# Attention and gated MLP on one core: row maxima ten pairs of units ahead instead of eleven, z's order in the rows, two pools for the gate

## The chip, the cores and the metric

The kernel runs on one core of one Trainium2 chip. The engines' names are those of the profile: PE is TensorE (its matrix products, PEld its weight loads), DVE is VectorE, ACT is ScalarE, POOL is GpSimd, SP is SyncE, from which most DMAs are issued. The metric is the device time of one execution in microseconds (us); the median of several runs is compared.

## The reference

```python
h = x + A(layernorm(x), wqkv, wo)
h2 = h + B(layernorm(h), w_in, w_sp, b_sp, w_out)

def A(x, wqkv, wo):                    # S=2048, D=512, 32 heads of Dh=16
    q, k, v = split(x @ wqkv)
    p = softmax(einsum("bhqd,bhkd->bhqk", q, k) * Dh ** -0.5)
    return einsum("bhqk,bhkd->bhqd", p, v) @ wo

def B(x, w_in, w_sp, b_sp, w_out):     # F=1376, Fh=688
    z = gelu(x @ w_in)
    z1, z2 = z[..., :Fh], layernorm(z[..., Fh:])
    g = einsum("ts,bsf->btf", w_sp, z2) + b_sp[None, :, None]
    return (z1 * g) @ w_out
```

Inputs and results are float32.

## The kernel before, in words

Most products in the projections and in the MLP are made of numbers split into a high and a low float16 part, and take three products (`mm3`, L108, L109, L110: high by high, high by low, low by high). In five engines' queues the order of instructions from the projections to the end of the rows is written by hand (`manual_schedule`): what stands behind a waiting instruction on its engine waits as well.

**Projections.** A loop of 24 projections of q and k (j = 0 to 23), twelve products each; the results are drained by VectorE (L461, L462). Into them are put the *row maxima* of the first scores. A softmax subtracts its row maximum before the exponential, and here the maxima are found from separate, smaller products, ahead of the scores: `max_pair(m)` makes eight steps, each one product (L224) into a bank of PSUM and an operation on it, six on VectorE alone (L229, one maximum each), and one pair of steps on ScalarE (absolute values, L234) and VectorE (L238). Eight m are a group of 512 queries of four heads. At its end `finish` reduces the group (L243) and splits it on GpSimd (L246 to L248), and `max_rows` turns it (L260), writes it to memory (L261, `m_scr`) and reads it back in two transfers (L264) into two rows of q, so that the scores' product subtracts the maxima. `ahead(k)` takes the next k steps during a projection, up to LEAD m in all.

**Attention.** There are 512 units (8 groups of four heads, 4 query blocks of 512, 16 key blocks), taken in pairs, 256 in all. Each pair follows the list `PAIR`: `s0` to `s7` are the eight score products (L801, in `product`), each with an exponential on ScalarE (L810); `M0` to `M7` are the eight steps of maxima for the pair that is LEAD pairs further on; `H` and `P` multiply weights by v (`weigh`, L826), for the pair before and the present one; `join` is `finish`, `turn` is `max_rows`, `out` copies a finished output from PSUM (`take`, L836), and `invert` makes the reciprocals of the sums. In the first pair there is nothing to weigh; four products with v as both operands (L1128, which the profile records as eight) stand there. The last LEAD pairs have no maxima left to make: the first of these follows `PAIR` without them, the others go through `scores2`, two products with one exponential of double width. Among these lie the beginnings of the next stage: rows of the output are loaded (`load_o`), scaled and split (`split_o`: ScalarE L735, VectorE L736), multiplied by wo (`make_h`, L743), 12 products one by one (`some_h`), and added to x (L747), with statistics (L750).

**Rows.** Sixteen rows of 128 positions in pairs (sb from the upper and the lower half). For each: `make_h` and `split_o` of later rows, `scale_h` and `minus_mean` (VectorE's small steps L754, L115 to L127, L764) for h of the row two further on; `make_z` four times (12 products of 344 columns each, L108 to L110, and a Gelu on ScalarE, L1206); `turn` transposes the next row (ScalarE L99, VectorE L105); statistics of z (L1268, L1219), and `gate_z` normalises z (L1222) and forms seven combinations of blocks for the gate. `parts` splits each of them into high (cast, L1210, ScalarE or GpSimd) and low (subtraction, L1211, VectorE or GpSimd).

**Gate and output.** The spatial product with w_sp is made from seven block products (A, C, B in turn; `product`, L108 to L110 with g). Their PSUM tiles come from one pool of four banks. ScalarE reads A with L1397 into p1 before t2 is added onto A. Then come the products with w_out.

Of the kernel before, what the change touches and what calls it, by code (L numbers as in the profile page):

```python
# [8 lines left out]
F32 = mybir.dt.float32  # L9
# [4 lines left out]
AF = mybir.ActivationFunctionType  # L14
# [18 lines left out]
KS = 48  # L33
LEAD = 11
KM = 50
PB = 6
FIRST = 2
RG = 64
# [21 lines left out]
def block_kernel(ctx: ExitStack, tc: tile.TileContext, x, wqkv, wo, w_in, w_sp4, b_sp, w_out, out):  # L60
# [209 lines left out]
    with ExitStack() as pre:  # L270
# [397 lines left out]
        for j in range(24):  # L668
            b, n, i = 1 + j // 8, j // 2 % 4, 1 - j % 2

            def between(d):
                if d == 1 and j >= FIRST:
                    ahead(5 if j < FIRST + 4 else 4)
                if d == 2 and takes:
                    takes.pop(0)()
                    if rest:
                        rest.pop(0)()
                if d == 3 and turned and done[0] % 8 > 3:
                    max_rows()
# [51 lines left out]

    def split_o(sb):
        o = os_.pop(sb)
        o2s[sb] = [e2.tile([P, DB, P], F16, name=f"o2{i}", bufs=1) for i in range(2)]
        nc.scalar.activation(o2s[sb][0], o, AF.Copy, scale=o_up)  # L735
        nc.vector.scalar_tensor_tensor(o2s[sb][1], o, o_up, o2s[sb][0], op0=ALU.mult, op1=ALU.subtract)  # L736
# [47 lines left out]
    with ExitStack() as at:  # L784
# [274 lines left out]
        for n in range(0, len(units), 2):  # L1059
# [38 lines left out]
            if len(later) == 2:  # L1098
                if turned:
                    max_rows()  # L1100
                more_h = n in (492, 494, 508, 510)
                scores2(hg, qb, kb, 0)
# [10 lines left out]
            for tok in PAIR if len(later) < 2 else ():  # L1113
# [10 lines left out]
                elif tok == "H" and prev is None:  # L1124
                    if first:
                        pv[0] = ps_v.tile([P, 512], F32, name="pv")
                        for j in range(4):
                            nc.tensor.matmul(pv[0][32 * j:32 * j + 32, :], vst[0][:, :32],  # L1128
                                             vst[0][:, :512], start=True, stop=True)
                    first = False  # L1130
                elif tok == "H":
# [12 lines left out]
            if len(later) == 2 and kb == 6:  # L1144
                invert()
            if n in (476, 480, 504, 508):
                asked.append(load_o(h_rows[{476: 0, 480: 1, 504: 2, 508: 3}[n]]))
            if n in (484, 488, 508):
                asked.pop(0)()
            if n in (488, 500, 510):  # L1150
                split_o(h_rows[(n - 488) // 11])
            if n == 500:
# [27 lines left out]
    with ExitStack() as mid:  # L1180
# [28 lines left out]
        def parts(name, k, src, eh, el):  # L1209
            (nc.gpsimd.tensor_copy if eh == "pool" else nc.scalar.copy)(T[name][0][:, k, :], src)  # L1210
            (nc.gpsimd if el == "pool" else nc.vector).tensor_sub(T[name][1][:, k, :], src, T[name][0][:, k, :])  # L1211

        def gate_z(sb, meanwhile):
# [28 lines left out]
            parts("t3", k, b12, "pool", "pool")  # L1242
            parts("b21", k, b21, "act", None)
            e.tensor_sub(t2, b21, t2)
# [3 lines left out]
        with tc.manual_schedule(engines={E.PE, E.Activation, E.DVE, E.Pool, E.SP}):  # L1248
# [3 lines left out]
            for k in range(NB):  # L1252
# [4 lines left out]
                if k + 3 < NB:  # L1257
                    split_o(row[k + 3])
                if new is not None:
                    mv, rs = scale_h(new)  # L1260
                    nb = minus_mean(e2, mv, rs)
                new_z(sb)
                make_z(sb, 1, 0)
                if k + 1 < NB:
                    turn(row[k + 1])
                make_z(sb, 1, 1)
                for c in range(2):
# [23 lines left out]
    with ExitStack() as fin:  # L1291
# [3 lines left out]
        ps_o = fin.enter_context(tc.tile_pool(name="fin_o", bufs=2, space=PSUM))  # L1295
        ps_g = fin.enter_context(tc.tile_pool(name="fin_g", bufs=4, space=PSUM))
        WB = len(FB) - 1
# [75 lines left out]
        with tc.manual_schedule(engines={E.PE, E.Activation, E.DVE, E.Pool, E.SP}):  # L1373
# [10 lines left out]
            for p in range(HB):  # L1384
# [5 lines left out]
                bt, bb = bias_up[:, p:p + 1], bias_up[:, p + HB:p + HB + 1]  # L1390
                A, C, B = [ps_g.tile([P, 512], F32, name="g")[:, :FC] for _ in range(3)]
                p1, v, q5 = [f2.tile([P, FC], F32, name=n) for n in ("p1", "v", "q5")]
# [73 lines left out]
```

## Time and profile before

| what | us |
|---|---|
| median of 3 runs (lowest, highest) | 1733.11 (1732.75, 1733.4) |
| the profiled execution's own time | 1732.66 |
| its span in the profile | 1730.9 |
| projections, 98 to 161.9 | 63.9 |
| first attention pair, to 167.46 | 5.56 |
| attention pairs with maxima, to 1250.25 | 1082.79 |
| the last 11 pairs, to 1295.57 | 45.32 |
| rows, to 1456.14 | 160.57 |
| gate and output, to 1731 | 274.86 |

Times in the rows of the profile count from the span's start. A timeline row has its start, its length, the engine, the line, the operation with output and inputs, and, in brackets, how long the engine was idle ahead of it and what ended that. A row of the groups view has line, engine, operation, shapes and count, then busy time in us and mean in ns, and the idle time ahead of the group with its cause. The windows view has start and end, length, and for each engine busy us and count of instructions, then the granted clock of PE (1.00 is full), the busy share of the DMA engines and GB/s. SPq is the queue of SP's DMAs.

### The profile page before, as it was taken

The numbers are of one execution on the slowest core, as the hardware profiler recorded it, in microseconds if no ns is written. First come the engines' busy times: TensorE is split into PE (matmuls) and PEld (weight loads), VectorE is DVE, ScalarE is ACT, GpSimd is POOL, SyncE is SP. The second block draws the span as 40 slices with busy tenths as digits, with TensorE's granted clock in tenths as the row PEclk, the third lists the DMA queues.
The fourth block names the chain that finished last, engine by engine and source line by source line (L and its number), as shares of the span: only waits on it lengthen the run. The fifth ranks groups of instructions, "written<-read, shape, count | busy, mean of one in ns | idle before, by whom it ended". The sixth has DMA issues, their size and how long they took to land.

```text
span 1730.9 us, 36558 instructions
## 1 busy us (share of the span) xinstructions
PE 1713.6 (99%) x13581; PEld 676.1 (39%) x13581; DVE 1389.4 (80%) x2896; ACT 1301.3 (75%) x2566; POOL 824.8 (48%) x1088
## 2 busy tenths in 40 slices
PE   9999999999999999999999999999999999999999
PEld 4433222222222222222222222222226666777776
DVE  7688999999999999999999999999927776111112
ACT  4334999999999999999999999999995554011000
POOL 1231867776672267877677767600004665100110
PEclk9999999999999999999999999999999999999999
DMA  5534332342231244445345434410125454743440
GB/s 183 162 97 143 101 88 74 98 100 73 75 71 29 63 124 134 139 125 150 92 141 139 133 111 128 108 23 9 45 58 143 131 172 149 274 148 132 171 173 25
DMA packets 185482, 196.13 MB, mean 113 GB/s; under 512 B 65960, under 2 KB 134632, under 8 KB 185304
## 3 DMA queue, kind: packets, MB, share of 16 engines
q1 hardware_dynamic: 183000, 188.16, 37.0%
q10 hardware_dynamic: 2304, 5.64, 0.9%
q8 instruction: 106, 1.74, 0.4%
q14 instruction: 72, 0.59, 0.1%
HBM read 124.92 MB, written 68.75 MB: 112 GB/s over the span
## 4 chain that ended last, share of the span: by engine, by line
PE 72%; DVE 15%; POOL 4%; ACT 3%; DMA 2%; issue 2%; SPq 1%; ACTq 0%; POOLq 0%; DVEq 0%
PE pv L826 24%; PE s L801 16%; PE m L224 9%; DVE mx L229 7%; PE g L108 4%; PE g L110 4%; PE g L109 4%; PE acc L108 3%; PE acc L110 3%; PE acc L109 3%; DMA rc<-r_scr 2%; DVE ab L238 1%; POOL op L1003 1%; ACT pt L810 1%; DVE og L836 1%
## 5 line engine op out<-in xcount | busy, mean ns | idle before, releaser
L810 ACT ACTIVATE pt<-s 128x512 f32<-128x512 f32 x1968 | 1006.9, 638 | 4.7 <-PE m L224 3.6
L229 DVE TENSOR_REDUCE mx<-m 128x1 f32<-128x512 f32 x1510 | 947.2, 682 | 12.8 <-PE m L224 3.9
L801 PE MATMUL s<-qst,kst 50*128 50x512 f16 x2048 | 604.4, 379 | 0.4
L826 PE MATMUL pv<-pt,vst 128*32 128x256 f32 (+1 forms) x6056 | 598.1, 466 | 4.1 <-DVE og L836 0.7
L224 PE MATMUL m<-kst,qst 48*128 48x512 f16 x1510 | 452.3, 381 | 0.0
L801 PEld LDWEIGHTS <-kst 50*128 50x128 f16 x2048 | 131.9, 94 | 352.1 <-issue 322.7
L826 PEld LDWEIGHTS pv<-pt,vst 128*32 128x32 f32 x6056 | 119.5, 108 | 289.9 <-issue 276.6
L224 PEld LDWEIGHTS <-qst 48*128 48x128 f16 x2048 | 159.3, 93 | 173.7 <-issue 123.8
L224 PE MATMUL m<-uvs,qst 48*128 48x512 f16 x504 | 190.7, 380 | 0.0
L238 DVE CUSTOM_DVE_ANT_0 ab<-m,ab 128x512 f32<-128x512 f32 x252 | 170.3, 676 | 2.7 <-ACT ab L234 2.7
L234 ACT ACTIVATE ab<-m 128x512 f32<-128x512 f32 x252 | 157.7, 626 | 16.5 <-PE m L224 15.8
L246 POOL TENSOR_SCALAR nm<-nm 128x16 f32<-128x16 f32 x32 | 6.5, 204 | 331.4 <-DVE nm L243 331.4
L1335 ACT ACTIVATE pT<-tp 128x384 fp32r<-128x384 f32 x32 | 14.0, 488 | 142.0 <-PE tp L1327 142.0
L1413 POOL TENSOR_TENSOR pr<-pr,z 128x344 f32<-128x344 f32 x8 | 7.3, 910 | 193.1 <-DVE pr L1412 181.7
L1003 POOL TENSOR_TENSOR op<-raw,op 128x512 f16<-128x512 f32 x80 | 92.8, 1160 | 5.8
L910 POOL TENSOR_TENSOR raw<-raw 128x512 f32<-128x512 f32 (+1 forms) x84 | 83.1, 989 | 6.7
L915 POOL TENSOR_TENSOR acc_sp<-acc_sp,raw 128x512 f32<-128x512 f32 x63 | 80.4, 1276 | 4.5
L110 PE MATMUL acc<-wi,hT 128*128 128x344 f16 x256 | 79.2, 309 | 2.1 <-DVE hT L105 2.1
L1357 DVE TENSOR_TENSOR y<-acc,h 128x512 f32<-128x512 f32 x16 | 11.1, 691 | 85.9 <-PE acc L1353 84.5
L108 PE MATMUL acc<-wi,hT 128*128 128x344 f16 x256 | 79.1, 309 | 0.0
L109 PE MATMUL acc<-wi,hT 128*128 128x344 f16 x256 | 79.1, 309 | 0.0
L907 POOL TENSOR_SCALAR raw<-raw 128x512 f32<-128x512 f32 (+1 forms) x88 | 52.1, 592 | 19.7 <-DMA raw<-in_wqkv 12.4
(227 smaller groups left out, 2269.3 us busy)
## 6 DMA issues: line engine op xcount, KB each, us to landing
raw<-in_w_sp SPq DMA_DIRECT2D x128, 256.0 KB
s_scr<-op SPq DMA_DIRECT2D x64, 256.0 KB
op<-s_scr SPq DMA_DIRECT2D x32, 512.0 KB
a_scr<-op SPq DMA_DIRECT2D x48, 256.0 KB
op<-a_scr SPq DMA_DIRECT2D x24, 512.0 KB
o_scr<-og SPq DMA_DIRECT2D x64, 128.0 KB
qst<-q_scr SPq DMA_DIRECT2D x192, 32.0 KB
kst<-k_scr SPq DMA_DIRECT2D x48, 128.0 KB
```

Of the source, the lines that this page charges most:

```text
L108: nc.tensor.matmul(ps, lh, rh, start=first, stop=False, **kw)
L109: nc.tensor.matmul(ps, lh, rl, start=False, stop=False, **kw)
L110: nc.tensor.matmul(ps, ll, rh, start=False, stop=last, **kw)
L224: nc.tensor.matmul(acc, q[r, p, c], keys[r, p], start=True, stop=True)
L229: nc.vector.reduce_max(at(t, e if t else e - 1), acc, axis=AX.X)
L234: nc.scalar.activation(ab[0], acc, AF.Abs)
L238: nc.vector.tensor_tensor_reduce(ab[0], acc, ab[0], 0.5, LOW, ALU.add, ALU.max, at(0, 0))
L801: nc.tensor.matmul(s, kst[hg % 2][r, p, kb * P:(kb + 1) * P], qst[hg * NQ + qb][r, p, :], start=True, stop=True)
L810: nc.scalar.activation(pts[p, kb][:, t, :], s, AF.Exp, scale=scales_[hg // 2])
L826: nc.tensor.matmul(pv[0][32 * j:32 * j + 32, a:b], vst[hg % 2][:, c:c + 32], pts[j % 2, kb][:, j // 2, a:b], start=kb == 0, stop=kb == NB - 1,
L910: pool.tensor_mul(got[0] if n else acc, got[0], got[0])
L1003: chores.append((lambda: pool.tensor_sub(t[0][:, 1], of(), t[0][:, 0]), TT))
```

## The change

LEAD falls from 11 to 10 and FIRST rises from 2 to 4; every projection from j = 4 on takes four steps of maxima (20 groups of four), where j = 2 to 5 took five and j = 6 to 22 four. One attention pair more has maxima, and one `scores2` pair less is there. The four products of v in the first pair are gone. The times at which the early rows are loaded, multiplied, split and made shift by a few units, the list of pairs that take an additional step of h has six places where it had four, and the split of three early rows is by VectorE (a tensor_scalar) where it was by ScalarE. In the rows, `scale_h` and `minus_mean` move behind the first `make_z` and the next row's `turn`; the subtraction for the low part of b21 is kept and issued there too, in the row after, except in the last. The gate takes its PSUM tiles from two pools of two banks in the order that the pool of four gave, but in other banks.

```diff
-LEAD = 11
+LEAD = 10
-FIRST = 2
+FIRST = 4
...
                 if d == 1 and j >= FIRST:
-                    ahead(5 if j < FIRST + 4 else 4)
+                    ahead(4)
...
-    def split_o(sb):
+    def split_o(sb, on_act=True):
...
-        nc.scalar.activation(o2s[sb][0], o, AF.Copy, scale=o_up)
+        if on_act:
+            nc.scalar.activation(o2s[sb][0], o, AF.Copy, scale=o_up)
+        else:
+            nc.vector.tensor_scalar(o2s[sb][0], o, o_up, None, op0=ALU.mult)
...
-                more_h = n in (492, 494, 508, 510)
+                more_h = n in (494, 496, 498, 500, 508, 510)
...
                 elif tok == "H" and prev is None:
-                    if first:
-                        pv[0] = ps_v.tile([P, 512], F32, name="pv")
-                        for j in range(4):
-                            nc.tensor.matmul(pv[0][32 * j:32 * j + 32, :], vst[0][:, :32],
-                                             vst[0][:, :512], start=True, stop=True)
-                    first = False
+                    pass
...
-            if n in (476, 480, 504, 508):
-                asked.append(load_o(h_rows[{476: 0, 480: 1, 504: 2, 508: 3}[n]]))
-            if n in (484, 488, 508):
+            if n in (474, 484, 504, 508):
+                asked.append(load_o(h_rows[{474: 0, 484: 1, 504: 2, 508: 3}[n]]))
+            if n in (484, 492, 508):
                 asked.pop(0)()
-            if n in (488, 500, 510):
-                split_o(h_rows[(n - 488) // 11])
+            if len(later) == 1 or n in (500, 510):
+                split_o(h_rows[max(n - 490, 0) // 10], False)
...
-            (nc.gpsimd if el == "pool" else nc.vector).tensor_sub(T[name][1][:, k, :], src, T[name][0][:, k, :])
+            sub = lambda e: e.tensor_sub(T[name][1][:, k, :], src, T[name][0][:, k, :])
+            if el == "later":
+                subs.append(sub)
+            else:
+                sub(nc.gpsimd if el == "pool" else nc.vector)
...
-            parts("b21", k, b21, "act", None)
+            parts("b21", k, b21, "act", None if last else "later")
...
-                if new is not None:
-                    mv, rs = scale_h(new)
-                    nb = minus_mean(e2, mv, rs)
                 new_z(sb)
                 make_z(sb, 1, 0)
                 if k + 1 < NB:
                     turn(row[k + 1])
+                if subs:
+                    subs.pop()(nc.vector)
+                if new is not None:
+                    mv, rs = scale_h(new)
+                    nb = minus_mean(e2, mv, rs)
                 make_z(sb, 1, 1)
...
-        ps_g = fin.enter_context(tc.tile_pool(name="fin_g", bufs=4, space=PSUM))
+        ps_g = [fin.enter_context(tc.tile_pool(name=f"fin_g{i}", bufs=2, space=PSUM)) for i in (1, 0)][::-1]
+        banks = [0]
+
+        def next_g():
+            banks[0] += 1
+            return ps_g[(banks[0] - 1) // 2 % 2].tile([P, 512], F32, name="g")[:, :FC]
...
-                A, C, B = [ps_g.tile([P, 512], F32, name="g")[:, :FC] for _ in range(3)]
+                A, C, B = [next_g() for _ in range(3)]
```

VectorE at the end of the projections, before (part is the drained result of a projection, mx a maximum, m and tp banks of PSUM):

```order
L462 SCALAR_TENSOR_TENSOR part<-acc,part 128x512
L229 TENSOR_REDUCE mx<-tp 128x1
L238 ISA ab,mx<-m_1791,ab 128x512
L238 ISA mx 128x1
L229 TENSOR_REDUCE mx<-m_1794 128x1
L462 SCALAR_TENSOR_TENSOR part<-acc,part 128x512 x2
L461 TENSOR_SCALAR part<-acc 128x512
L462 SCALAR_TENSOR_TENSOR part<-acc,part 128x512
L229 TENSOR_REDUCE mx<-m_1902 128x1
```

and in the change:

```order
L462 SCALAR_TENSOR_TENSOR part<-acc,part 128x512
L229 TENSOR_REDUCE mx<-m_1776 128x1
L238 ISA ab,mx<-tp,ab 128x512
L238 ISA mx 128x1
L229 TENSOR_REDUCE mx<-tp 128x1
L462 SCALAR_TENSOR_TENSOR part<-acc,part 128x512
L461 TENSOR_SCALAR part<-acc 128x512
L462 SCALAR_TENSOR_TENSOR part<-acc,part 128x512
L229 TENSOR_REDUCE mx<-m_1877 128x1
```

The last group of maxima now stands one drain (L462) further back: between it and the first maximum of the attention (m_1902, m_1877) are three drain operations where four were.

TensorE in the first attention pair, before (qst, uvs and kst hold q and k, vst v; s a score, m a bank for a maximum, pv the weighted v):

```order
L224 LDWEIGHTS qst
L224 MATMUL m_1912<-kst_164,qst 128x512
L801 LDWEIGHTS kst_164
L801 MATMUL s<-qst,kst_164 128x512
L1128 MATMUL pv<-vst_162 32x512 x4
L801 LDWEIGHTS kst_164
L801 MATMUL s<-qst,kst_164 128x512
L224 LDWEIGHTS qst
L224 MATMUL m_1926<-kst_164,qst 128x512
```

and in the change:

```order
L224 LDWEIGHTS qst
L224 MATMUL m_1887<-kst_164,qst 128x512
L804 LDWEIGHTS kst_164
L804 MATMUL s<-qst,kst_164 128x512
L804 LDWEIGHTS kst_164
L804 MATMUL s<-qst,kst_164 128x512
L224 LDWEIGHTS qst
L224 MATMUL m_1896<-kst_164,qst 128x512
```

Only the four products that took v as both operands are gone; the scores and the maxima keep their order.

VectorE in a row of the third stage, before (b is a block of z for the gate, xr the row of h, hT the transposed row's low part):

```order
L764 TENSOR_SCALAR nb<-rs_u,zmv 128x1
L1211 TENSOR_TENSOR b_1_20715<-z_21879,b_0_20714 128x344
L747 SCALAR_TENSOR_TENSOR xr<-acc,fig_1851,xr 128x512
L750 BN_STATS st<-xr 128x6
L736 SCALAR_TENSOR_TENSOR o_22015<-o,fig_1850,o_22014 128x512
L754 BN_AGGR mv<-st 128x2
L115 TENSOR_SCALAR rs_v_22020<-mv 128x1
```

and in the change:

```order
L767 TENSOR_SCALAR nb<-rs_u,zmv 128x1
L750 SCALAR_TENSOR_TENSOR xr<-acc,fig_1826,xr 128x512
L753 BN_STATS st<-xr 128x6
L739 SCALAR_TENSOR_TENSOR o_22021<-o,fig_1825,o_22020 128x512
L105 TENSOR_TENSOR hT_22047<-tp,hT_22046 128x512
L1209 TENSOR_TENSOR b_1_20722<-z_21868,b_0_20721 128x344
L757 BN_AGGR mv<-st 128x2
L115 TENSOR_SCALAR rs_v_22053<-mv 128x1
```

The subtraction for b21 (L1211, now L1209) stood ahead of h's sum (L747, now L750), and L105 behind the whole scale of h, which begins with L754 (now L757); now L105 comes directly behind the split of o, with the subtraction and then the scale of h behind it.

More of the change, by code (lines that the diff above doesn't have):

```diff
@@ L1210, in parts @@
             (nc.gpsimd.tensor_copy if eh == "pool" else nc.scalar.copy)(T[name][0][:, k, :], src)
-            (nc.gpsimd if el == "pool" else nc.vector).tensor_sub(T[name][1][:, k, :], src, T[name][0][:, k, :])
+            sub = lambda e: e.tensor_sub(T[name][1][:, k, :], src, T[name][0][:, k, :])
[3 more added lines that the diff above has]
+                sub(nc.gpsimd if el == "pool" else nc.vector)
+        subs = []
         def gate_z(sb, meanwhile):
```

## The prediction

> **What bounds the kernel now.** I read the page's first section first, then the windows view with one stretch for each stage (columns: sum, then busy time and count of PE, DVE, ACT and POOL with PE's weight loads second, granted clock, DMA share, GB/s).
>
> ```profile
> span 1730.9 us, 36558 instructions
> PE 1713.6 (99%) x13581; PEld 676.1 (39%) x13581; DVE 1389.4 (80%) x2896; ACT 1301.3 (75%) x2566; POOL 824.8 (48%) x1088
> ```
>
> ```profile
>   167.46:1250.25 1082.79, 1078.72 (x9764) 306.53 (x9761) 1074.15 (x2084) 1081.50 (x2198) 657.60 (x862) 1.00 0.35 96
>   1295.57:1456.14 160.57, 157.32 (x1004) 98.11 (x1002) 125.83 (x407) 83.23 (x145) 97.60 (x116) 1.00 0.47 144
>   1456.14:1731.00 274.86, 270.42 (x1712) 191.70 (x1712) 52.22 (x106) 28.98 (x61) 27.67 (x43) 1.00 0.43 155
> ```
>
> TensorE is busy 99% of the span, so an edit is worth what it takes from TensorE's work or from its few gaps. In the long stage (244 pairs of units, 1082.79/244 = 4.44 us each) VectorE and ScalarE are as full as TensorE; nothing can be hidden there, but the change leaves the order inside such a pair alone. In the rows TensorE lacks 3.25 us, behind the gate's start 4.44. The clock is 1.00 in all three. So I went to the timeline at each place which the change touches. The sum is made against the profiled execution, 1732.66 us: its span 1730.9 and 1.8 around it; the median of the runs is 0.45 above it.
>
> **The projections: five maxima units in a group become four.** One pair's maxima, eight units, leave this stage.
>
> ```profile
> 101.80 0.60 PE L224 MATMUL m<-kst,qst 48*128 48x512 f16 x3
> 105.25 0.39 PE L224 MATMUL m<-kst,qst 48*128 48x512 f16 x1
> 108.48 0.39 PE L224 MATMUL tp<-kst,qst 48*128 48x512 f16 x1
> 153.62 0.69 DVE L238 CUSTOM_DVE_ANT_0 ab<-tp,ab 128x512 f32<-128x512 f32 x1 [1.93 <-ACT ab L234]
> 153.77 0.39 PE L224 MATMUL m<-kst,qst 48*128 48x512 f16 x2
> 157.38 0.39 PE L224 MATMUL tp<-kst,qst 48*128 48x512 f16 x1
> 159.22 0.38 PE L108 MATMUL acc<-xT,wqk 128*128 128x512 f16 x1
> 161.59 0.38 PE L110 MATMUL acc<-xT,wqk 128*128 128x512 f16 x1
> ```
>
> Eleven steps of product lie between the last two rows, so a product costs 2.37/11 = 0.2155 us, and a projection of twelve 2.59. The step from 101.80 to 105.25 is the last with five units, 3.45; the next, with four, 3.23. Four units cost 3.23 − 2.59 = 0.64, the fifth 0.22. The change puts one group of four less (0.64) and four fifth units less (0.88): −1.52. One step of four, 153.77 to 157.38, took 3.61, 0.38 over the others: VectorE's running maximum had waited 1.93 for ScalarE's absolute values, which stand behind the register loads at j = 20. With groups of four from j = 4 on, that half of a unit pair falls on another j, and the wait has what ScalarE needs. I take −1.9, with bounds −1.5 (the 0.38 stays) and −1.9.
>
> **The first attention pair: the stand-ins.**
>
> ```profile
> 162.01 0.69 DVE L461 TENSOR_SCALAR part<-acc 128x512 f16<-128x512 f32 x1 [0.50 <-PE acc L110]
> 163.34 3.67 DVE L229 TENSOR_REDUCE mx<-m 128x1 f32<-128x512 f32 x6
> 163.58 1.06 PE L1128 MATMUL pv<-vst 128*32 128x512 f32 x8 [0.85 <-DVE part L462]
> 167.46 0.39 PE L801 MATMUL s<-qst,kst 50*128 50x512 f16 x1
> ```
>
> The last product ends at 161.59 + 0.22 = 161.81 = E, and the second pair's first score starts at E + 5.65, though a steady pair takes 4.44. The stand-ins hold 1.06 of it, but TensorE isn't what is late: this pair's six maxima (3.67 us, 0.61 each) start on VectorE only when the three drain operations of the last projection are through. Taking the stand-ins out leaves that chain. It even grows: the last projection has a group of maxima of its own now (j runs on to 23), so VectorE has that group's three operations ahead of the three drain operations, where in the order listing two of the drain's stood before. From their lengths the first reduction starts about E + 2.3, where it was E + 1.53; the other steps keep the pitch of 0.61. My count for the second pair's first score is E + 6.1: **+0.45**. Bounds: −1.06 (all stand-ins on the path) does not fit the 3.67 behind them, so 0, and +0.8 if the whole shift of the first reduction comes through.
>
> **The last pairs without maxima: ten, not eleven, and the early rows' split on VectorE.**
>
> ```profile
> 1250.25 0.39 PE L801 MATMUL s<-qst,kst 50*128 50x512 f16 x1
> 1255.23 0.39 PE L801 MATMUL s<-qst,kst 50*128 50x512 f16 x2
> 1263.09 0.61 PE L801 MATMUL s<-qst,kst 50*128 50x512 f16 x4
> 1264.94 0.39 PE L801 MATMUL s<-qst,kst 50*128 50x512 f16 x2
> 1275.49 0.39 PE L743 MATMUL h<-wo,o 128*128 128x512 f16 x1 [0.64 <-ACT o L735]
> 1278.51 0.55 DVE L760 TENSOR_SCALAR hn<-xr,mv,rs_u 128x512 f32<-128x512 f32 x1
> 1296.57 0.59 PE L743 MATMUL acc<-wo,o 128*128 128x512 f16 x2 [0.35 <-DVE og L836]
> ```
>
> Before: one pair in the old order without maxima (1250.25 to 1255.23, 4.98: ScalarE's split, 0.77 us by my estimate from its like, stands among the exponentials), then ten pairs as twenty halves of 1.85 us (1263.09 to 1264.94); 24 products of h lie in them, of which four are additional ones (more_h) at 0.2155; and 0.64 for h's wait on ScalarE's split. Sum 4.98 + 37.00 + 0.86 + 0.64 = 43.48. After: one pair more with maxima, 4.44; the pair without, 4.40, since the split has left ScalarE; eighteen halves, 33.30; six additional products, 1.29; and about 0.5 for the wait on the split, which now stands on VectorE behind the early row's sum and statistics (its price there by L760, the nearest tensor by scalars, 0.55). Sum 43.93, so +0.45. Against it stands 0.25 of the 0.35 for the last copy of the output (L836): VectorE has nothing ahead of it there. I take **+0.2**, bounds −0.4 (h doesn't wait) to +0.6.
>
> **The rows: z's order and the late subtraction.**
>
> ```profile
> L110 PE MATMUL acc<-wi,hT 128*128 128x344 f16 x256 | 79.2, 309 | 2.1 <-DVE hT L105 2.1
> 1343.97 0.52 DVE L1211 TENSOR_TENSOR b<-z,b 128x344 f16<-128x344 f32 x1 [1.92 <-ACT b L1210]
> 1347.00 0.17 DVE L754 BATCH_NORM_AGGREGATE mv<-st 128x2 f32<-128x6 f32 x1
> 1349.39 0.68 DVE L105 TENSOR_TENSOR hT<-tp,hT 128x512 f16<-128x512 f32 x1
> 1350.13 0.32 PE L110 MATMUL acc<-wi,hT 128*128 128x344 f16 x1 [0.37 <-DVE hT L105]
> 1370.88 0.32 PE L110 MATMUL acc<-wi,hT 128*128 128x344 f16 x1 [0.37 <-DVE hT L105]
> ```
>
> The groups view says that the third product of z waited 2.1 us in all for the transposed row's low part (L105), five times 0.37 and once 0.28; the last two rows show it twice, two rows of work (20.75 us) apart. On VectorE that instruction stands behind the scale of the next h (1347.00 to 1349.39, 2.39 us of small steps) and, in every second row, behind the subtraction for b21, which idles 1.92 for ScalarE's cast. The change puts both behind L105. So it comes up to 2.39 + 1.92 earlier, where 0.37 is needed: **−2.1**, all of it. What is late next: the scale of h is wanted by ScalarE's hn at the row's end, some 7 us (24 products of 0.31) further on, so it has cover; without that cover the same 0.37 returns at the next transposition. VectorE's own pace has room: 125.83 busy of 160.57. Bounds: −2.1 and +0.4.
>
> **The gate's banks.**
>
> ```profile
> 1456.14 0.31 PE L108 MATMUL g<-b,op 128*128 128x344 f16 x1 [0.79 <-POOL t L1210]
> 1462.58 0.52 DVE L1211 TENSOR_TENSOR n<-t,n 128x344 f16<-128x344 f32 x1 [0.54 <-ACT n L1210]
> 1463.26 0.55 ACT L1397 ACTIVATE p<-g,fig 128x344 f32<-128x344 f32 x1 [0.71 <-DVE n L1211]
> 1463.85 0.31 PE L108 MATMUL g<-t,op 128*128 128x344 f16 x1 [0.56 <-ACT p L1397]
> ```
>
> The gate's first product waits 0.79. The profile names POOL, but the waits in the program say that it is the bank: the first one lay where the last z had been, until its Gelu was read out. With two pools the first product gets banks of the transpositions, long free, and 0.79 goes. But the second product on A waits until p1 has been read from A (L1397), and p1 stands until VectorE's last subtraction (1462.58 + 0.52) has ended. If that stays, the gap of 0.56 becomes 0.56 + 0.79 = 1.35 and nothing is won. VectorE's chain at the last rows should come earlier, because its 1.92 is gone from the rows ahead: by my estimate the A product starts 7.3 us behind the last z's end, where it was 1463.85 − 1455.35 = 8.5. So I take **−1.1**, with bounds 0 and −1.35.
>
> The Trainium skill, "TensorE: Matmul & The Clock Gate", Part 1 (The HAM clock gate), says that TensorE falls to half its clock after an idle window of about 3.4 us. The gaps that I move are 0.4 to 1.4 us and the granted clock beside those of before was 1.00, so by that rule nothing is added.
>
> **The row maxima, one pair later.** Maxima of a pair group go out to memory and come back as two rows of q before the scores that subtract them.
>
> ```profile
> 331.54 0.33 SPq L261 DMA_DIRECT2D m_scr<-mturned  x1
> 332.95 1.32 SPq L264 DMA_DIRECT2D qst<-m_scr  x2
> 340.30 0.39 PE L801 MATMUL s<-qst,kst 50*128 50x512 f16 x1
> GB/s 0 0 0 0 0 0 0 0 0 0 0 0 0 0 0 0 0 0 13 11 9 12 9 1 0 0 0 10 11 11 11 9 139 27 82 109 137 164 164 164
> ```
>
> The write is issued at 331.54, the first read when it has landed, 1.41 later, and the DMA view (window 333 to 336, slices of 0.075 us) shows the reads' small packets at 334.35 to 334.8 and 335.0 to 335.4. The first score, at 340.30, needs the first read; the other read is wanted by a score 0.6 later. So the slack is 340.30 − 334.8 = 5.5 for the first and as much for the second; one pair takes 4.44 of it, the signal behind the packets by my estimate 0.3, and about **0.8 us** is left. There are 31 such groups. Most should fit; one (near 1148 us, where other traffic is heavy) I expect some 0.4 late. I take +0.2, bounds 0 and the second rival.
>
> The Trainium skill, "DMA: Bandwidth & Descriptors" (Anatomy of one DMA — SWDGE path), counts about 2.0 us fixed for a transfer, most of it the receipt. The row shows 1.41 for the write; by the page's figure write and read would be half a microsecond longer together, and would still just fit.
>
> **Sum.** −1.9 + 0.45 + 0.2 − 2.1 − 1.1 + 0.2 = −4.25: 1728.4 in an execution like the profiled one, and 0.45 more, **1728.9 us**, as the median.
>
> **The rivals.** *VectorE still sets the rows' pace.* The waits on L105 are short because VectorE's chain just misses; if moving it makes z's statistics late, ScalarE's normalised z, and with it the last subtraction in front of p1, come no earlier. Then a third of the 2.1 and none of the gate's 1.1 is had: −4.25 + 1.4 + 1.1 = −1.75, **1731.4**. For it: VectorE's idle in the rows is 34.74 us in many pieces, each ended by ScalarE; against it: TensorE is the fuller engine there.
> *The row maxima land late* (the other side): a slack of 0.8 us in each of 31 groups. It decides once the chain from a group's reduction to the landed rows is 0.8 longer than in the group shown; each 0.1 beyond costs 31 × 0.1 = 3.1 us. With 0.4 in every group it is 12.4 − 4.25 = +8.15, **1741.3**. For it: 4.7 of 5.5 are used; against it: the shown group stands for its like, and most groups' packets are small.
> *The join nearer to the output's copy.*
>
> ```profile
> 1252.13 0.21 DVE L243 TENSOR_REDUCE nm<-mx 128x16 f32<-128x64 f32 x1
> ```
>
> VectorE has (1082.79 − 1074.15)/244 = 0.035 us idle in a pair; the join's reduction (0.21) and the turning now come one pair nearer to the copy of the output, which VectorE also pays off over several pairs. If one 0.21 in each group comes through to TensorE: 31 × 0.21 − 4.25 = +2.25, **1735.4**; if half, 1732.1. Against it: a group's eight pairs have the same work in any order, and the lag is paid off by the end of a group either way.
> *The gate's pools only move the wait:* 1.1 is lost, **1730.0**; for it speaks p1's wait on VectorE. *The first pair's gap costs clock:* TensorE's waits at the attention's start add up to some 2 us; one period at half speed there costs up to 1.7, **1730.6**.
>
> **How the numbers follow.** Forecast 0.53 (its own range 1727.4 to 1730.3, from the terms' bounds not all at one end), VectorE's pace 0.19, late maxima 0.12, the gate's pools 0.07, the join 0.06, the clock 0.03. The likeliest gives 1728.9. The range from 1727.0 to 1733.0 holds the forecast, three rivals and half of the join, and leaves out the late maxima and the rest. A measurement tells 0.2%, 3.47 us, from no change: faster is below 1729.64. That holds nine tenths of the forecast and a part of the gate's and the clock's cases, 0.52; slower, above 1736.6, is the late maxima and a remainder, 0.13; the same 0.35.
>
> **What would show it.** Right: steps of 3.2 in all projections and none of 3.6; about E + 6.1 to the second pair's first score; an idle time near zero before L105's product in the rows; the gate's first gap gone and the second not above 0.6; pairs of 4.44 on the mean, as before. Wrong: first scores of groups that wait for a DMA (late maxima), first pairs of groups above 4.6 with VectorE named (the join), a gap of 1.35 before the second product on A (pools), or waits of z on VectorE or ScalarE elsewhere in the rows.

## The result, and the profile after

| | before | changed |
|---|---|---|
| median of 10 runs (us) | 1732.99 | 1738.16 |
| lowest to highest | 1732.6 to 1733.4 | 1736.49 to 1741.5 |
| ratio to before | | 1.0032 [1.0023, 1.0041] |

The change makes the kernel slower by 5.2 us (0.3%), where 4 us less were forecast, and its executions lie 5 us apart where those of before lie within 1. The profiled execution is the slowest of the ten (1741.5), 8.8 us longer than the one before; it shows all that can go wrong, not what goes wrong each time.

The first section of the page, and TensorE's timeline at the end of the projections and in the first two pairs (start, length, engine, line, operation; in brackets the idle time ahead and what ended it; `...` stands for rows left out):

```profile
span 1739.7 us, 36541 instructions
PE 1720.1 (99%) x13581; PEld 677.4 (39%) x13581; DVE 1395.6 (80%) x2899; ACT 1300.7 (75%) x2567; POOL 825.7 (47%) x1088
```

```profile
159.53 0.38 PE L110 MATMUL acc<-xT,wqk 128*128 128x512 f16 x1
160.99 0.37 PE L804 MATMUL s<-qst,kst 50*128 50x512 f16 x1 [1.08 <-issue]
...
164.06 0.58 PE L224 MATMUL m<-kst,qst 48*128 48x512 f16 x1 [0.20 <-DVE mx L229]
...
167.03 0.60 PE L804 MATMUL s<-qst,kst 50*128 50x512 f16 x1
```

The last product of the projections ends at 159.53 + 0.22 = 159.75, 2.06 earlier than before. The second pair starts at 167.03, 7.28 behind it, where it was 5.65 and 6.1 was forecast. From 164.06 on the same products take 0.58 to 0.60 and not 0.38. The windows view says why (the column behind the engines is the granted clock):

```profile
160.00:163.00 3.00, 1.68 (x10) 0.63 (x11) 2.97 (x6) 1.60 (x4) 0.00 (x0) 1.00 0.63 196
163.00:167.00 4.00, 3.57 (x15) 0.42 (x13) 3.40 (x7) 2.92 (x6) 0.00 (x0) 0.59 0.57 188
167.00:170.00 3.00, 3.00 (x22) 0.62 (x18) 1.89 (x3) 1.58 (x3) 2.62 (x4) 0.50 0.96 315
172.00:174.00 2.00, 2.00 (x14) 0.20 (x8) 1.89 (x4) 1.57 (x3) 1.75 (x4) 0.51 0.58 127
174.00:176.00 2.00, 2.00 (x22) 0.56 (x18) 1.19 (x2) 1.22 (x3) 1.83 (x3) 1.00 0.54 137
```

TensorE is busy 1.68 of the 3 us up to 163, and from a little before 164 it runs at half its clock until 174. In the long stage the same happens once more, at the first pair of group 4:

```profile
306.23 1.07 PE L829 MATMUL pv<-pt,vst 128*32 128x512 f32 x8
308.18 0.39 PE L804 MATMUL s<-qst,kst 50*128 50x512 f16 x1 [0.89 <-DMA qst<-m_scr]
...
309.47 0.39 PE L804 MATMUL s<-qst,kst 50*128 50x512 f16 x1 [0.47 <-DMA qst<-m_scr]
```

Two scores wait for the row maxima, and the clock is 0.50 from 311 to 313. Then the rows and the gate, from the groups view (idle time and its cause in the last column) and the timeline:

```profile
L110 PE MATMUL acc<-wi,hT 128*128 128x344 f16 x256 | 79.1, 309 | 0.0
L1189 PE MATMUL tp<-ident,hn 128*128 128x128 f32 x60 | 9.3, 277 | 1.9 <-ACT hn L1280 1.9
```

```profile
1443.98 0.69 DVE L105 TENSOR_TENSOR hT<-tp,hT 128x512 f16<-128x512 f32 x1 [1.09 <-ACT hT L99]
1444.59 0.17 DVE L757 BATCH_NORM_AGGREGATE mv<-st 128x2 f32<-128x6 f32 x1
...
1446.37 0.31 PE L110 MATMUL acc<-wi,hT 128*128 128x344 f16 x1
1446.85 0.21 DVE L767 TENSOR_SCALAR nb<-rs_u,mv 128x1 f32<-128x1 f32 x1
1447.10 0.81 ACT L1280 ACTIVATE hn<-xr,nb,rs_u 128x512 f32<-128x512 f32 x1 [1.58 <-DVE nb L767]
1447.96 0.65 PE L1189 MATMUL tp<-ident,hn 128*128 128x128 f32 x4 [1.28 <-ACT hn L1280]
...
1469.74 0.52 DVE L1209 TENSOR_TENSOR n<-t,n 128x344 f16<-128x344 f32 x1 [0.54 <-ACT n L1208]
1470.42 0.55 ACT L1409 ACTIVATE p<-g,fig 128x344 f32<-128x344 f32 x1 [0.71 <-DVE n L1209]
1471.02 0.44 PE L108 MATMUL g<-t,op 128*128 128x344 f16 x1 [3.09 <-ACT p L1409]
```

The wait on L105 is gone, as forecast; a wait of TensorE on hn has come in its place. The first gap of the gate is gone too, and the second has grown from 0.56 to 3.09. Behind it the products take up to 0.49 (half clock) until 1474.4. So the 8.8 us of this execution, stage by stage, from such rows in both traces (a last product of the projections is counted to its start + 0.22, the end of z to the last product's start + 0.31):

| from, to | before | after | difference | forecast |
|---|---|---|---|---|
| start to the last projection product | 161.81 | 159.75 | −2.06 | −1.9 |
| to the third pair's first score | 10.06 | 14.60 | +4.5 | +0.45 |
| to the 241st pair's first score | 1056.12 | 1059.78 | +3.7 | +0.2 |
| to the first h product of the rows | 68.58 | 68.84 | +0.3 | +0.2 |
| to the end of z | 158.78 | 157.96 | −0.8 | −2.1 |
| to the second product on A (the gate's two gaps) | 8.50 | 10.09 | +1.6 | −1.1 |
| to the end | 267.05 | 268.68 | +1.6 | 0 |

### The profile page after: what moved, and what is told of

Its sections match the earlier page's. It is cut to its first block, busy times and chain, and to the rows that moved or that the text cites. A ratio compares the mean times of both kernels' runs of the same rounds, so it can differ in the third digit from the quotient of the medians.

```text
span 1739.7 us, 36541 instructions
## 1 busy us (share of the span) xinstructions
PE 1720.1 (99%) x13581; PEld 677.4 (39%) x13581; DVE 1395.6 (80%) x2899; ACT 1300.7 (75%) x2567; POOL 825.7 (47%) x1088
## 3 DMA queue, kind: packets, MB, share of 16 engines
q10 hardware_dynamic: 2304, 5.64, 0.8%
q8 instruction: 106, 1.74, 0.4%
## 4 chain that ended last, share of the span: by engine, by line
PE 78%; DVE 13%; DMA 3%; ACT 2%; POOL 2%; issue 1%; SPq 1%; ACTq 0%; DVEq 0%; POOLq 0%
PE pv L829 26%; PE s L804 18%; PE m L224 10%; DVE mx L229 6%; PE g L108 4%; PE g L109 4%; PE g L110 4%; PE acc L108 3%; PE acc L110 3%; PE acc L109 3%; DMA rc<-r_scr 1%; DVE ab L238 1%; DVE og L839 1%; DVE rs_t L125 1%; DVE rs_u L127 1%
## 5 line engine op out<-in xcount | busy, mean ns | idle before, releaser
L108 PE MATMUL g<-t,op 128*128 128x344 f16 x192 | 60.1, 313 | 3.1 <-ACT p L1409 3.1
```

The lines of the kernel that those rows point to most:

```text
L108: nc.tensor.matmul(ps, lh, rh, start=first, stop=False, **kw)
```

## The experiments

Each was timed beside the kernel before on the same chip (its medians there 1733.2 to 1733.3).

| run | median, us | lowest to highest | ratio to before, 95% |
|---|---|---|---|
| changed kernel + products of v | 1734.64 | 1733.25 to 1736.05 | 1.0009 [1.0000, 1.0018] |
| changed kernel + scale of h in front | 1730.66 | 1729.29 to 1732.69 | 0.9987 [0.9978, 0.9996] |
| before + z's order | 1733.93 | 1733.81 to 1734.21 | 1.0005 [0.9996, 1.0014] |
| before − products of v | 1733.52 | 1732.05 to 1735.99 | 1.0000 [0.9991, 1.0009] |
| changed kernel + both | 1728.18 | 1727.36 to 1728.71 | 0.9970 [0.9959, 0.9982] |
| changed + scale + turn earlier | 1729.32 | 1728.48 to 1731.7 | 0.9978 [0.9969, 0.9987] |
| changed + both + turn earlier | 1727.73 | 1727.2 to 1728.58 | 0.9969 [0.9956, 0.9981] |
| before + the gate's pools | 1733.29 | 1732.12 to 1734.07 | 1.0001 [0.9992, 1.0010] |
| changed + 37 products at the start | 1736.46 | 1735.02 to 1738.9 | 1.0021 [1.0012, 1.0030] |
| changed + both + 37 products | 1730.21 | 1727.64 to 1731.53 | 0.9982 [0.9973, 0.9991] |
| changed + both, groups from j = 3 | 1727.21 | 1727.16 to 1727.71 | 0.9966 [0.9952, 0.9979] |
| before + late b21 + the gate's pools | 1728.15 | 1727.77 to 1728.5 | 0.9971 [0.9959, 0.9982] |

### The products of v back in the first pair

```diff
                 elif tok == "H" and prev is None:
-                    pass
+                    if first:
+                        pv[0] = ps_v.tile([P, 512], F32, name="pv")
+                        for j in range(4):
+                            nc.tensor.matmul(...)
+                    first = False
```

> The changed kernel with the four products of v put back into the first attention pair, nothing else. Theory A (without them TensorE has too little work in the first pair, and its clock is halved for some 10 us from 164 us on, which cost about 4 us beside my +0.45): granted clock 1.00 from 161 to 175 us, the second pair's first score about 6 us after the last projection product, time about 4 us under the changed kernel's 1738.2, so near 1734. Rival (the added group of maxima at j = 23 holds VectorE back and the clock falls anyway): clock still 0.5 there, time within 1 us of 1738.2.

1734.64: 3.5 us less, as the first theory has it. In the windows view of this kernel, against the first three rows above:

```profile
160.00:163.00 3.00, 1.37 (x12) 0.44 (x14) 2.96 (x6) 1.42 (x3) 0.00 (x0) 1.00 0.70 222
163.00:167.00 4.00, 3.88 (x31) 1.03 (x24) 3.71 (x8) 3.19 (x8) 0.00 (x0) 1.00 0.58 177
167.00:170.00 3.00, 3.00 (x34) 0.97 (x34) 2.90 (x5) 3.00 (x8) 2.51 (x4) 1.00 0.99 326
```

Full clock, though VectorE's chain is the same and TensorE is even less busy up to 163. But the clock isn't all of the 3.5 us: between the third and the 241st pair this profile takes 1056.14, 3.6 less than the change's. The gate's gap of 3.09 is there as in the change, here without a half clock behind it.

### The scale of h back in front

```diff
+                if new is not None:
+                    mv, rs = scale_h(new)
+                    nb = minus_mean(e2, mv, rs)
                 new_z(sb)
                 make_z(sb, 1, 0)
...
                 if subs:
                     subs.pop()(nc.vector)
-                if new is not None:
-                    mv, rs = scale_h(new)
-                    nb = minus_mean(e2, mv, rs)
```

> The changed kernel with the scale of h (and minus_mean) back in front of z's first products; the late subtraction for b21 and the gate's pools stay. Theory A (the scale of h behind the transposition makes hn late, this makes the next transposition late, and the chain of the last rows with it, so that p1 comes late in the gate): no waits on hn in the rows, no wait of 0.37 on the low part either, the second gap of the gate falls from 3.1 to between 0.6 and 1.4 with no half clock behind it, time about 4 us below 1738.2. Rival (the two pools let the gate run into p1 earlier, and the gap is theirs): gap still near 3 us, time at most 1.3 lower.

1730.66, 7.5 us less, more than expected. This kernel's groups view and timeline:

```profile
L1189 PE MATMUL tp<-ident,hn 128*128 128x128 f32 x60 | 9.0, 272 | 0.0
1462.56 0.31 PE L108 MATMUL g<-t,op 128*128 128x344 f16 x1 [1.03 <-ACT p L1409]
```

No wait in the rows at all, and 1.03 at the gate. From the second to the sixteenth row's transposition it takes 137.78 us; before it was 141.59, after 140.65. So the edit gives 2.9 in the rows and 2.1 in the gate's gap, and the half clock behind that gap (1.6 in the change's profile) doesn't come. The pools were in this kernel, so the gap was not theirs.

### z's order alone, on the kernel before

Its edit is the change's part in the loop over rows and in `parts`, both shown with the change.

> The kernel before with z's order alone (scale of h moved back, subtraction for b21 late). Theory A: waits on hn of 0.2 in the rows and over 1 us at the last transposition, the gate's gaps together about 0.8 + 2.5, perhaps with a half clock behind them: 1734 to 1736, slower than before. Rival of the prediction (z's order is a gain and the gate's pools spoil it): 1731, with the gate's gaps as before.

1733.93, slightly above before (the interval holds 1) and just under what was expected; no gain. What the late subtraction wins in the rows, the later scale of h loses again, as this timeline shows:

```profile
1442.37 0.66 PE L1191 MATMUL tp<-ident,hn 128*128 128x128 f32 x4 [1.28 <-ACT hn L1282]
1456.33 0.31 PE L108 MATMUL g<-b,op 128*128 128x344 f16 x1 [0.99 <-POOL z L1234]
1465.41 0.31 PE L108 MATMUL g<-t,op 128*128 128x344 f16 x1 [1.92 <-ACT p L1405]
```

The same 1.28 on hn, and gaps of 0.99 and 1.92 where 0.79 and 0.56 were.

### The kernel before without the products of v

```diff
                 elif tok == "H" and prev is None:
-                    if first:
-                        ...
-                    first = False
+                    pass
```

> The kernel before without the four products of v in the first pair, nothing else. Theory A: the clock falls to half from about 164 us on, 3 to 4 us slower than before, near 1736.5. Rival (only the shorter lead's other order at the end of the projections does it): clock 1.00, within 0.5 us of 1733.0, since VectorE's maxima, not the products, set the pair's end.

Missed by the median: 1733.52, no difference, but the executions spread over 4 us (those of before, timed beside them, over 2.5). The profiled one is the slowest (1735.99) and has the half clock (windows view):

```profile
163.00:167.00 4.00, 3.09 (x14) 0.69 (x17) 4.00 (x7) 4.00 (x9) 0.00 (x0) 0.86 0.45 134
167.00:170.00 3.00, 3.00 (x18) 0.48 (x14) 1.70 (x5) 0.96 (x3) 1.66 (x2) 0.50 0.92 301
```

The mean granted clock is below 1.0 (0.998 or 0.999) in seven of the eleven runs, and in three of the 33 of before. So with the longer lead the products keep away a loss that comes in part of the executions and not in others. With the shorter lead, where the start has one more gap, it comes nearly always, as the runs with the turn earlier show further down.

### Both back in the changed kernel

> The changed kernel with both: the scale of h back in front (1730.7 in its run) and the four products of v back in the first pair. Theory A (these products keep the clock up at the start): 1.00 at 161 to 175 us, time 1 to 3 us under 1730.7, so 1727.7 to 1729.7. Rival (with the scale of h back, the start is no matter any more; what the products cost, about 1 us of TensorE, eats the gain): 1730 to 1731.5.

1728.18, in the range of the theory and 2.5 below the scale of h alone; the clock is 1.00 throughout the start. The two repairs take 10.0 us off the change. Again the 2.5 us are not the clock alone: in the two profiles the way from the last projection product to the third pair differs by 0.95 (11.85 without the products, 10.90 with them), the long stage behind it by 2.66 (1059.07 and 1056.41).

### The row maxima's turn three steps earlier

```diff
-PAIR = "s0 M0 join s2 M4 M1 s1 H s3 invert M2 s5 M3 H out M5 s4 M7 turn s6 s7 M6 P".split()
+PAIR = "s0 M0 join s2 M4 M1 s1 H s3 invert M2 s5 M3 turn H out M5 s4 M7 s6 s7 M6 P".split()
```

Without the products of v:

> The changed kernel with the scale of h back in front, and the row maxima's turn and transfers three steps earlier in the pair (turn behind M3 and not behind M7, so about 1.2 us earlier). No products of v. Theory T (the slack of 0.8 us is used up in the groups whose write takes long, and their scores wait for the reads): the waits at the first pairs of groups 4 to 16, 2.95 us in the trace with the scale back alone, go or fall below 0.5; time 1.5 to 2.5 us under 1730.7. Rival (the turn waits on VectorE for GpSimd's parts and holds up the maxima behind it, 0.1 to 0.3 us in each of 32 groups): pairs with a turn get longer, 1733 or more.

and with them:

> All three: the changed kernel with the scale of h back in front, the products of v back in the first pair, and the turn three steps earlier. If the three causes are separate and add up: no half clock at the start, no waits for the row maxima, one gap of about 1 us in the gate; 1726.5 to 1728, below both kernels. If they overlap (the late groups are late only because the start was): as with the products of v alone, 1728 to 1729.5.

1729.32 and 1727.73: 1.3 us less than without the move, where 1.5 to 2.5 were expected, and 0.45 less, which is within the spread of the runs. In neither profile does the timeline show a score that waits for the reads, and the pairs of the first keep their lengths. So these two kernels price the products of v by themselves: 1.6 us, with a mean granted clock of 0.997 to 0.999 in all eleven runs without them and of 1.0 in all six with them. But the move doesn't buy the time by which it is earlier. SP's timeline of the second kernel and of the change, at group 4:

```profile
298.21 0.33 SPq L261 DMA_DIRECT2D m_scr<-mturned  x1
301.77 1.37 SPq L264 DMA_DIRECT2D qst<-m_scr  x2
```

```profile
302.88 0.33 SPq L261 DMA_DIRECT2D m_scr<-mturned  x1
305.91 1.37 SPq L264 DMA_DIRECT2D qst<-m_scr  x2
```

The reads are issued when the write has landed: 3.56 and 3.03 us later, where 1.41 is usual. The DMA view of the change from 302 to 306.5 shows who else is there, beside the 144 small packets of the write and one read:

```profile
q1 hardware_dynamic: 144, 0.01, 1.9%
q8 instruction: 1, 0.02, 1.3%
```

One fetch of instructions, 16 KB. At group 5, whose write takes 1.41, the view has no such line. By the trace's semaphore events the write lands in 16 parts, as many as there are DMA engines; 14 or 15 of them are done after 1.2 to 1.4 us, and one or two are late. The trace doesn't say which DMA engine a packet took; that the late part shares one with the fetch is inferred. Over all fourteen traces, groups 1 to 31 (434 writes), counted from the packets (fetches of 16 KB and, on another queue, of 8 KB):

```
                                        write below 1.55 us   over 1.55 us
no instruction fetch that starts -0.6
to +1.1 us from the write's issue                338                0
such a fetch                                      17               79
```

The stretch of -0.6 to +1.1 was read off the first ten traces; in the last four, made later, all 19 late writes lie in it too. The fetches on q8 are 106 of 16 KB, 1.74 MB; TensorE has 2 × 13581 instructions, 64 bytes each by that division. A pair of units has 80 of them, 16 pairs are five such fetches, so they fall on the same place of every second group for a long while.

### The fetches moved

```diff
-        stay_warm(30)
+        stay_warm(27)
+        for _ in range(40):
+            nc.tensor.matmul(warm[:, :4], idle[:, :P], idle[:, :4], start=True, stop=True)
```

In the changed kernel:

> The changed kernel with 37 products more at its very start (27 of the 30 warming products and 40 with 4 columns), in a gap of TensorE, so that TensorE's instruction fetches of 16 KB fall some 4 us earlier in each pair of groups. Theory F (a write of the row maxima is late when such a fetch holds one of its 16 DMA engines: in all traces so far the writes over 1.6 us behind group 0 are those with a fetch between -0.6 and +1.1 us of their issue): no write of groups 1 to 20 over 1.6 us but those with the other, 8 KB fetches; the waits for the reads, 1.6 us and a half clock behind them in the profile of the change, go; median 2 to 3 us under 1738.2 and the runs closer together than the 5 us of the change. Rival (the loads for w_sp or the buffer of even groups make it late): the same even groups 4 to 16 stay late, time within 0.7 us of 1738.2.

and with the two repairs:

> The kernel with the products of v and the scale of h back (1728.2 in its run), with the same 37 products more at the start. Theory F: the writes of groups 2 to 10, 1.8 to 2.3 us in that kernel's profile, come to 1.4 to 1.5, and its waits of about 0.6 us together go: 1727.2 to 1728. Rival: nothing changes, or the added products cost their time, 1728.2 to 1729.

In the first, only the writes of groups 13 and 26, with 8 KB fetches, are still over 1.55, and the long stage is down from 1059.78 to 1056.17 (profiles of the change's slowest and of this kernel's fastest execution). The median is 1.7 lower, less than expected: the half clock at the start and the gate's gap stay, and so does most of the spread. The second is a miss in the other direction: 2.0 us slower. There the even groups up to 24 are on time, and the fetch, which drifts a little from group to group, arrives in the odd groups from 21 on:

```profile
904.25 0.33 SPq L261 DMA_DIRECT2D m_scr<-mturned  x1
907.62 1.33 SPq L264 DMA_DIRECT2D qst<-m_scr  x2
```

```profile
q1 hardware_dynamic: 144, 0.01, 2.5%
q8 instruction: 1, 0.02, 1.9%
```

(SP's timeline and the DMA view from 904 to 908.) Two scores wait 1.13 each there, and the long stage takes 1058.94 where it took 1056.41. The late writes follow the fetch into other groups, which neither the loads nor the buffer would do.

### Groups of maxima from j = 3

```diff
-FIRST = 4
+FIRST = 3
```

> The kernel with the products of v and the scale of h back, and the twenty groups of maxima from j = 3 to 22 and not 4 to 23, so that the last projection has none. Theory (the group at j = 23 delays VectorE's drain and so the second pair, which starts 6.5 us behind the last product and not 5.65 as before): second pair's first score at 5.6 to 5.8 us behind, 0.8 us off 1728.2, 1727.2 to 1727.7. Rival (the start is set by the pair's own six maxima): 6.4 us, no change.

1727.21, the fastest of all. The last product and the second pair's first score:

```profile
160.08 0.38 PE L110 MATMUL acc<-xT,wqk 128*128 128x512 f16 x1
...
165.94 0.39 PE L804 MATMUL s<-qst,kst 50*128 50x512 f16 x1
```

165.94 − 160.30 = 5.64, as before the change: the group at j = 23 cost the 0.85.

### The gate's pools alone, and with the late subtraction

> The kernel before with the gate's two pools alone. Rival R5 of the prediction (the wait only moves to p1): first gap 0.8 gone, second 1.35, time within 0.3 us of before. The prediction's term (chain comes earlier) doesn't apply without z's order, so a gain above 0.5 us would say that p1's wait isn't on VectorE's last subtraction.

1733.29: nothing. The first gap is gone, the second is 1.50 (0.79 + 0.56 = 1.35 was expected), and from the end of z to the second product on A it takes 8.50 as before.

> The kernel before with the late subtraction for b21 and the gate's two pools; lead, stand-in products and the scale of h as before. Theory: the rows' pairs come down from 20.73 to 20.06 us as in the change with the scale of h back, 3.8 us over the stage, the gate loses its first gap and has about 1.2 at p1: 1729 to 1729.6, so that the shorter lead with all that belongs to it is worth about 1 us on top (1728.2). Rival (the rows' gain needs the other lead's timing): above 1731.

1728.15, better than expected, with eleven pairs of lead. So the late subtraction and the pools, with the scale of h left where it was, are worth 5.0 us, and the shorter lead with the products put back adds nothing to that (1728.18); with the groups from j = 3 it adds 0.9.

## Why the prediction was wrong

Two steps failed, and they explain the distance to the forecast: with the scale of h and the products of v put back, the changed kernel takes 1728.2 where 1728.9 was forecast for the change itself. That this comes so near is partly luck: in that profile the start costs 0.85 for the 0.45 forecast and the gate gives 0.5 for 1.1, and the rows make up for it with 3.8 for 2.1.

**"The scale of h is wanted by ScalarE's hn at the row's end, some 7 us further on, so it has cover."** This is the larger one, 7.5 us in the medians. The cover is shorter: VectorE's scale now waits behind L105, which itself waits for ScalarE's cast of the transposed row (idle 1.09 ahead of it at 1443.98). The 2.47 us of small steps begin behind it, at 1444.59, hn waits 1.58 for them, and the next transposition waits for hn, 0.2 in three pairs of rows and 1.28 at the last. There TensorE has work up to 1446.37 + 0.15 = 1446.52, which is 1.93 behind 1444.59; the small steps and hn's 0.81 want 3.28, and the transposition starts at 1447.96, 1.44 late. By the run with the scale of h in front, the gap at p1 hangs on this too. The prediction asked what is late next and named hn, but took its length of cover from TensorE's products and not from the instructions that VectorE would have to finish; and it counted 24 products at 0.31, their length in the profile, where they follow each other every 0.146, which makes 3.5 us and not 7. The rival with VectorE setting the pace had the right place, at 0.19, but let the gate only lose its gain: the measured gate lost 1.6, and a half clock behind it another 1.6.

**"Taking the stand-ins out leaves that chain", at a cost of 0.45.** The chain was about right: E + 6.1 was forecast, and 6.49 is measured with the products put back, where the clock stays up. What was left out is that the products kept the clock up. The clock was among the rivals at 0.03 and 1.7 us; the pair of kernels with the turn earlier, where no score waits for the maxima, puts it at 1.6 us in the medians (1729.32 to 1727.73). In the change's profile the start lost more, 3.7 (14.6 to the third pair against 10.9 with both repairs). The 2.5 us from 1730.66 to 1728.18 hold late row maxima too: group 4's write takes 3.35 us in the one profile and 2.30 in the other. That the instructions of the products shift the fetches is a likely reason, not one that was tested alone.

The prediction reasoned with single gaps of up to 1.4 us. The Trainium skill, "TensorE: Matmul & The Clock Gate", Part 1 (The HAM clock gate), names an idle window of about 3.4 us ahead of the half clock. Here the longest single wait ahead of it was 1.08, and TensorE was busy over half of the time around it; so the measurement decides, and the clock also falls without such a window. How busy TensorE was in one stretch doesn't settle it either: 1.68 of the 3 us to 163 in the change, and only 1.37 with the products put back, where the clock stayed. What does settle it stays open.

**The gate.** That the pools only move the wait (rival, 0.07) is what the run of the pools alone shows. The forecast 1.1 needed an earlier chain. With the scale of h in front the chain is earlier, but from the end of z to the second product on A it still takes 8.03 where it was 8.50, a gain of about 0.5.

**The row maxima.** The slack of 0.8 us was right for the mean write, but the price of 31 groups for each 0.1 was not: not all groups are a little late, but some by much, those whose write meets an instruction fetch (in the change eight, at 1.66 to 3.03 us). The slow write of before that the prediction put down to other traffic (2.55 us, issued at 1148.26) met one as well. In the profile of the change the late groups cost 3.7 with the half clock; in the median, by the run with the fetches moved, about 1.7.

**What held.** The projections gave 2.06 for 1.9 (1.87 between the means of the traces that share the one or the other order there). The tail was +0.3 for +0.2. L105's waits went, and here the size was off the other way: 3.8 us are had, not 2.1, when nothing takes their place. The idle column said 0.37 for each; but the row before it shows why that is too little:

```profile
1390.97 0.31 PE L109 MATMUL acc<-wi,hT 128*128 128x344 f16 x1
1391.64 0.32 PE L110 MATMUL acc<-wi,hT 128*128 128x344 f16 x1 [0.36 <-DVE hT L105]
```

(TensorE's timeline before.) Products follow each other every 0.146 us, so 1391.64 − 1390.97 − 0.146 = 0.52 was lost, where the row says 0.36; the idle time counts from the modelled end of a product, 0.31 behind its start, and a wait below 0.16 isn't seen in it at all. A pair of rows came down from 20.75 to 20.06, by 0.69 where 0.37 was counted; 0.15 of it was lost ahead of a product of h (L743, at 1388.65), with no idle time shown there.

## What to carry to other kernels

A step of small instructions that is moved out of one engine's way has a consumer: count the cover in that engine's own queue up to the consumer's due time, not in the work of the engine it was meant to help. A filler product in a start-up phase may look idle and off the path and still hold the clock, so try its removal alone and look at the spread of the runs. Where a transfer has little slack, look for the slowest one of its kind and at what it meets, since the mean write says little; and for a pipelined engine take waits from the starts of instructions, not from the idle column.

## What the runs showed of the hardware

Instruction fetches hold up the kernel's own transfers: a small write of 16 parts landed 0.2 to 2.2 us late in 79 of the 96 cases in which a fetch of 16 or 8 KB started beside it, and in none of the 338 without one; of the 79, 72 had a single late part and seven had two. Thirty-seven products that compute nothing of use took this loss away in one kernel (median −1.7) and put it into other groups in the next (+2.0). TensorE's clock fell to 0.50 for some 3 to 10 us after stretches in which it was still busy over half of the time, and after one wait of 3.09; it stayed at 1.00 after the same wait in another run, and in one start with TensorE busy less than half of 3 us, so the runs don't give the condition.
